# Own maxima for the last four pieces, a first load in halves, and a new step order in the prologue of an attention-plus-PReLU kernel

## The chip, the core and the metric

The kernel runs on one core of one Trainium2 chip. The metric is the device time of one execution in microseconds (us), the median of several runs. A core has five engines that work side by side, each through its own queue in program order: TensorE (PE: matrix products and transposes), VectorE (DVE), ScalarE (ACT), GpSimd (POOL), and SyncE (SP), which here only issues DMA transfers. 16 DMA engines move the data. Matrix products land in PSUM, from where DVE or ACT copy them to SBUF; POOL does not touch PSUM in this kernel.

## The reference

Two layers, one after the other. The first is attention through 32 learned rows I ("inducing"), for each of 4 batches of 12480 rows of 128 floats:

```python
def mab(q, kv):
    s = scale * (q @ kv.transpose(0, 2, 1))
    s = s - s.max(-1, keepdims=True)
    a = np.exp(s)
    a /= a.sum(-1, keepdims=True) + 1e-09
    return a @ kv
h = mab(I, x)       # 32 rows per batch, a softmax over all 12480 rows of x
y = mab(x, h)       # every row of x against these 32 rows
```

The second takes the 49920 rows of y through `h = y @ w_in` (128 to 2048 columns), `g = max(h, 0) + alpha * min(h, 0)`, and `g @ w_out` (2048 to 128). Inputs and output are float32; the kernel computes its products in bf16. The softmax of the first `mab` runs over a whole batch, so nothing of y can be computed for a batch before all of its 12480 rows have been read.

## The kernel before, in words

**Phase A and phase B.** Phase A of a batch is `h = mab(I, x)`. Phase B is everything after it for that batch: the second attention and the two products, in one main loop over blocks of 512 rows, four "visits" of 4 x 128 columns of w_in to each block (`visit`, `second`, `linear`, `finish`, L791 to L903). The main loop does phase B of batch b and, between its products, phase A of batch b + 1; a planner (`Plan`) settles before the build which of ACT and DVE does which evacuation. Only phase A of batch 0 has nothing to hide under. It is the **prologue**: an order of steps written out by hand (the string `order`, L1117 to L1125), which `begin` (L1045) carries out one by one. Every step puts its instructions at the end of the queue of the engine that it uses, so the string fixes the order on each engine.

**Pieces.** Batch 0 is read in eight pieces (`first_pieces`): piece 0 is 16 tiles of 128 rows, piece 1 the short rest of 192 rows, pieces 2 to 5 are 16 tiles each, and pieces 6 and 7 are the two halves (8 tiles each) of the last 16. A buffer holds 16 tiles (1 MB of float32) and there are four buffers (`xs`, bufs=4). The first five pieces are loaded at once; the load of piece 5 waits for the buffer of piece 0, those of pieces 6 and 7 for that of piece 2. The loads of `w_in` and `w_out` (1 MB each, `load_weights`, L1031) take the buffers of pieces 3 and 4. In `load_weights` a small POOL memset of two columns stands ahead of the load of `w_in` (L1033); the load waits for it, and it stands in POOL's queue behind the first POOL cast of piece 5.

**Steps of a piece p**, in the letters of the string, with a trailing a, v or p for ACT, DVE or POOL:

- `kp.i`: cast part i of the piece to bf16 (L347, L349; the short piece L335).
- `tp.i`, `cp.i`: transpose that part on PE (L364) and copy it from PSUM (L370, L372).
- `sp`: the scores of the piece against I (L379). `mp` (`a_least`, L388): one DVE scan negates and scales the scores and accumulates their minimum into column p of `mx` (L393), and a reduce over columns 0 to p gives the running minimum in column p of `rm` (L402).
- `ep` (`a_exp`, L413): ACT's exponential with `rm[p]` as bias, its sum in `da[p]`. `fp` (`a_fac`): the factor exp(rm[p] - rm[p-1]) on ACT (L436).
- `up`, `vp`: transpose the exponentials back (L456) and copy them (L462, L464).
- `hp`: PE's product with the piece (L473). `gp` (`a_add`, L483): DVE adds it to the running sum: hs = hs * fac[p] + product (L489).

After the last piece: `mg`, `rb`, `mm`, `mf` join the four groups of 32 partitions (L508, L517, L524/L525, L531); `ex` (`a_worth`, L544) gives each piece's weight exp(rm[last] - rm[p]), `dn` (`a_total`, L554/L555) the denominator, `pd`, `rec` its reciprocal (L568, L573/L574), `ph`, `hT` the result h transposed (L583, L588). From there the first block of phase B is made ready: `b`, `bm`, `bs`, `be`, `bt`, `ba` are scores, maximum, difference, exponential, transpose and copy of the first four tiles (L645, L676, L680, L774, L780, L788); `w`, `hw` are h times w_in (L599, L606); `b2`, `rx`, `rl`, `rk`, `re` do the scores of the other twelve tiles. Then visit 0 begins (L809, followed by `second`, L835).

**Weights.** `kwp` casts w_in on POOL (L1076). Right at that step SP's transpose of it, `winT` (L1135), is issued, and eight POOL products are queued: four make W1 from w_out (L974), which `second` needs, and four make AW (L983), which `linear_product` (L993) needs at visit 5. Batch 1's first loads follow `winT` in SP's queue.

**Zero products.** `Wn` and `warm(n)` (L956) put n products of a blank tile into PE's queue, 128x256 in bf16, each into a PSUM bank that nobody reads; 34 of them come before the first piece's transposes, 44 stand in the string.

**Banks.** `ring` gives the prologue's PSUM tiles out of six banks in turn.

## Time and profile before

| | |
|---|---|
| median of 3 runs | 592.18 us (592.09 to 592.28) |
| the profiled execution's own time | 592.11 us |
| span of its trace, first to last instruction | 590.3 us |
| granted TensorE clock over the span | 0.999 |
| PE's products over the whole span, `second` (L835) | 417.2 us |
| PE's products over the whole span, `visit` (L809) | 155.4 us |
| bytes moved over the span | 80.56 MB |

The trace is of one execution; all its times are counted from the first instruction. A row of the timeline gives the start, the duration, the engine, the line, the operation, the tiles written and read, their shapes and the number of merged instructions; a bracket at its end is the time that the engine sat idle before it and what ended that time. A merged row's duration runs from the first start to the last end. A row of the windows gives for each engine the busy time in a stretch, then the granted clock, the mean busy share of the 16 DMA engines, and the GB/s that they moved.

### The profile page before, as it was taken

To read this page: it belongs to the slowest core of one execution; us is meant where nothing else is said; L and a number is where in the kernel's file an instruction comes from. 1 tells how busy PE (TensorE), PEld (TensorE's weight loads), DVE (VectorE), ACT (ScalarE), POOL (GpSimd) and SP (SyncE) were. 2 spreads that over 40 slices of the span, in tenths; PEclk is the share of its full clock that TensorE was granted. 3 is DMA by queue.
4 is the path that set the end of the run, shared out by engine and by line. 5 is a ranking of instruction groups with operands and counts; after the bars stand their busy time and mean duration, and the time that the engine had idled before them with its cause. 6 is when DMAs were issued, how large, how long until landed. Compare 5 with 4: busy or idle time off the path is not lost.

```text
span 590.3 us, 23123 instructions
## 1 busy us (share of the span) xinstructions
PE 582.9 (99%) x9492; PEld 440.0 (75%) x9492; DVE 535.0 (91%) x979; ACT 537.6 (91%) x1087; POOL 217.1 (37%) x262
## 2 busy tenths in 40 slices
PE   9999999999999999999999999999999999999997
PEld 6577777777777777777777777777777777777776
DVE  5899999988998999999999899999999999999996
ACT  5799999999999999999999999999998998999986
POOL 3485552523325525413326256124034134144110
PEclk9999999999999999999999999999999999999999
DMA  8968699532188999332258899531331341433421
GB/s 336 276 181 176 158 250 197 132 98 73 39 240 159 209 216 222 94 95 58 78 152 181 194 255 204 136 100 38 92 77 50 92 81 49 118 85 57 92 69 47
DMA packets 122411, 80.56 MB, mean 136 GB/s; under 512 B 103824, under 2 KB 106176, under 8 KB 119232
## 3 DMA queue, kind: packets, MB, share of 16 engines
q1 hardware_dynamic: 122080, 78.99, 55.3%
q8 instruction: 74, 1.21, 0.8%
q14 instruction: 33, 0.27, 0.2%
q10 hardware_dynamic: 224, 0.09, 0.1%
HBM read 28.07 MB, written 25.56 MB: 91 GB/s over the span
## 4 chain that ended last, share of the span: by engine, by line
PE 95%; DMA 3%; DVE 1%; DVEq 0%; ACT 0%; issue 0%; POOL 0%; SPq 0%
PE bp L835 66%; PE hh L809 22%; DMA xs<-in_x_dram 3%; PE bp L862 2%; PE hh L645 2%; PE hh L473 1%; PE hh L379 1%; PE bp L960 0%; PE hh L364 0%; PE hh L599 0%; DVEq L1366 0%; PE hh L456 0%; DVE xn L349 0%; PE hh L583 0%; DVE hs L489 0%
## 5 line engine op out<-in xcount | busy, mean ns | idle before, releaser
L822 ACT ACTIVATE gt<-hh 128x512 bf16<-128x512 f32 x854 | 455.3, 606 | 34.4 <-PE hh L809 29.5
L824 DVE TENSOR_SCALAR gt<-hh 128x512 bf16<-128x512 f32 x706 | 453.7, 684 | 24.0 <-PE hh L809 13.6
L835 PE MATMUL bp<-W,gt 128*128 128x128 bf16 x6240 | 417.2, 220 | 0.7 <-DVE gt L824 0.7
L835 PEld LDWEIGHTS <-gt 128*128 128x128 bf16 x6240 | 349.4, 98 | 84.6 <-issue 76.0
L809 PE MATMUL hh<-a,HW 32*128 32x512 bf16 (+2 forms) x1664 | 155.4, 370 | 0.0
L759 POOL TENSOR_TENSOR rep<-e,rc 128x2048 bf16<-128x2048 f32 (+2 forms) x26 | 84.8, 3265 | 23.0 <-DVE rc L750 22.6
L727 POOL TENSOR_TENSOR e<-e,smx 128x512 f32<-128x512 f32 (+1 forms) x24 | 24.6, 1026 | 154.7 <-ACT gt L822 83.5
L809 PEld LDWEIGHTS <-HW 32*128 32x128 bf16 x1664 | 40.4, 91 | 41.6 <-issue 5.8
L713 POOL TENSOR_TENSOR t<-e 128x256 f32<-128x256 f32 (+1 forms) x24 | 17.2, 718 | 142.5 <-ACT e L689 142.5
L888 ACT COPY ob<-bp 128x512 f32<-128x512 f32 (+1 forms) x63 | 36.9, 586 | 4.5 <-PE bp L835 1.4
L713 POOL TENSOR_TENSOR t<-t 128x128 f32<-128x128 f32 (+3 forms) x100 | 30.5, 305 | 7.8
L330 POOL CAST xn<-xs 128x2048 bf16<-128x2048 f32 x17 | 32.1, 1890 | 0.8 <-DMA xs<-in_x_dram 0.3
L890 DVE COPY ob<-bp 128x512 f32<-128x512 f32 x31 | 21.3, 686 | 5.2 <-PE bp L835 5.2
L393 DVE TENSOR_SCALAR_CACHE_REDUCE s<-hh 128x512 f32<-128x512 f32 (+2 forms) x29 | 18.0, 619 | 1.6 <-PE hh L379 1.6
L862 PEld LDWEIGHTS <-a 32*128 32x128 bf16 x392 | 15.0, 93 | 5.7
L862 PE MATMUL bp<-HA,a 32*128 32x128 bf16 x392 | 19.1, 214 | 0.0
L418 ACT ACTIVATE e1T<-s,rm 128x512 bf16<-128x512 f32 (+1 forms) x25 | 18.0, 719 | 0.3
L722 DVE TENSOR_REDUCE smx<-e 128x16 f32<-128x512 f32 (+1 forms) x24 | 15.9, 662 | 0.0
L689 ACT ACTIVATE e<-e 128x512 f32<-128x512 f32 (+1 forms) x24 | 15.0, 624 | 0.0
L960 PE MATMUL bp<-blank 128*128 128x256 bf16 x78 | 13.6, 308 | 1.2 <-DVE blank L910 1.2
L489 DVE SCALAR_TENSOR_TENSOR hs<-hs,fac,hh 128x128 f32<-128x128 f32 (+1 forms) x25 | 8.6, 344 | 5.9 <-PE hh L473 5.2
L703 ACT COPY e<-hh 128x512 f32<-128x512 f32 (+1 forms) x22 | 13.4, 609 | 0.0
(107 smaller groups left out, 202.1 us busy)
## 6 DMA issues: line engine op xcount, KB each, us to landing
out_dram<-ob SPq DMA_DIRECT2D x97, 256.0 KB, 2.6
xs<-in_x_dram SPq DMA_DIRECT2D x23, 1024.0 KB, 6.1
xs<-in_x_dram SPq DMA_DIRECT2D x2, 512.0 KB, 9.2
w_in_f<-in_moe_w_in_dram SPq DMA_DIRECT2D x1, 1024.0 KB, 4.8
a<-rep SPq DMA_TRANSPOSE x27, 4.6
xT<-xn SPq DMA_TRANSPOSE x18, 5.7
e<-e1T SPq DMA_TRANSPOSE x18, 3.6
xs_left<-in_x_dram SPq DMA_DIRECT2D x4, 64.0 KB, 5.0
```

Source lines behind the costliest of these rows:

```text
L330: nc.gpsimd.tensor_copy(out=st.xn[s][:], in_=xs[:])
L393: nc.vector.tensor_scalar(out=s1[:parts, :cols], in0=ps[:parts, :cols], scalar1=-scale, scalar2=None, op0=MULT, op1=MIN, accum_out=st.mx[: ...
L713: nc.gpsimd.tensor_tensor(out=t[:, :n], in0=src[:, :n, :w], in1=src[:, :n, w : 2 * w], op=ADD)
L727: nc.gpsimd.tensor_tensor(out=st.e2[s][:, :n], in0=st.e2[s][:, :n], in1=st.m2[s][:, :n].unsqueeze(2).broadcast_to([P, n, M]), op=SUB,)
L759: nc.gpsimd.tensor_tensor(out=st.rep[s][:, ts], in0=st.e2[s][:, ts].unsqueeze(2).broadcast_to([P, n, R, M]), in1=rc[:, ts].unsqueeze(2).un ...
L809: nc.tensor.matmul(hh[:, q * cols + w.start : q * cols + w.stop], HWs[b][rows, v * P : (v + 1) * P], a2[rows, t0 : t0 + nt, :].rearrange(" ...
L822: nc.scalar.activation(out=gt[:, :cols], in_=hh[:, :cols], func=RELU)
L824: nc.vector.tensor_relu(gt[:, :cols], hh[:, :cols])
L835: nc.tensor.matmul(blk.acc[:, t * C : (t + 1) * C], gt[:, (q * nt + t) * P : (q * nt + t + 1) * P], W1[:, k, :], start=(not blk.begun), st ...
L862: nc.tensor.matmul(blk.acc[w, t * C : (t + 1) * C], blk.a2[rows, blk.t0 + t, w], HAs[b][rows, :], start=(not blk.begun and t == 0), stop=F ...
L888: nc.scalar.copy(out=ob[:, :nt], in_=acc)
L890: nc.vector.tensor_copy(out=ob[:, :nt], in_=acc)
```

## The change

- Pieces 4 to 7 of batch 0 (`own`) no longer take the running minimum: the scan's minimum goes straight into `rm[p]`, and the reduce over the columns is not issued for them. A new step `ml` (`a_lowest`) takes the minimum of `rm[3]` to `rm[7]` once, into `lo`. The factors `f4` to `f7` are gone; `g4` to `g7` use ex[p], the weight against `lo`, as factor of the new product instead of a factor of the sum, and a new step `gs` (`a_scale`) multiplies the sum of pieces 0 to 3 by ex[3] once, on POOL. `g4` to `g7` thus come after `ml` and `ex`. `dn` writes its products to a tile of its own (`dx`).
- Piece 0 is loaded in two halves, the second half first.
- The short piece is 2 x 96 rows in place of 128 + 64: one load and one cast in place of two of each, in every batch. Scores and exponentials of a piece take a view with a third dimension for it.
- The small memset ahead of the load of w_in is gone; the two loads of weights are issued at a new step `lw`.
- Zero products: a float32 blank of 512 columns. Ahead of the first piece's transposes stand two products of 512 columns and one of 384, each one instruction in the source; in the string stand one of 256, two of 128 and one of 256 columns (`W2`, `W1`, `W1`, `W2`).
- The eight POOL products of the weights are queued after the last step instead of at `kwp`; `winT` stays at `kwp`.
- The whole string is new.

```diff
@@ a_load
-            ts = slice(pc.t0, pc.t0 + pc.n)
-            nc.sync.dma_start(out=st.xs[s][:, ts], in_=rows[:, ts])
+            cut = pc.t0 + (H if not (st.b or pc.k) else 0)
+            for ts in (slice(cut, pc.t0 + pc.n), slice(pc.t0, cut)):
+                if ts.start < ts.stop:
+                    nc.sync.dma_start(out=st.xs[s][:, ts], in_=rows[:, ts])
...
+    def own(st, p):
+
+        return not st.b and p >= EARLY
+
+    def a_lowest(st):
+        nc.vector.tensor_reduce(
+            out=st.lo[:], in_=st.rm[:, EARLY - 1 : st.np], axis=AX, op=MIN
+        )
+
+    def a_scale(st):
+
+        nc.gpsimd.tensor_tensor(
+            out=st.hs[:],
+            in0=st.hs[:],
+            in1=st.ex[:, EARLY - 1 : EARLY].broadcast_to([P, C]),
+            op=MULT,
+        )
@@ a_least
-                accum_out=st.mx[:parts, p : p + 1],
+                accum_out=(st.rm if own(st, p) else st.mx)[:parts, p : p + 1],
             )
-            nc.vector.tensor_reduce(
-                out=st.rm[:, p : p + 1], in_=st.mx[:, : p + 1], axis=AX, op=MIN
-            )
+            if not own(st, p):
+                nc.vector.tensor_reduce(
+                    out=st.rm[:, p : p + 1], in_=st.mx[:, : p + 1], axis=AX, op=MIN
+                )
@@ a_add
+            elif own(st, p):
+                nc.vector.scalar_tensor_tensor(
+                    out=st.hs[:],
+                    in0=ps[:],
+                    scalar=st.ex[:, p : p + 1],
+                    in1=st.hs[:],
+                    op0=MULT,
+                    op1=ADD,
+                )
@@ blank and warm
-    blank = const.tile([P, 2 * P], bf16, name="blank")
-    for t in (xn_left, blank, e1T_left):
+    blank = const.tile([P, BT * P], f32, name="blank")
+    for t in (blank, xn_left, e1T_left):
...
-    def warm(n):
+    def warm(*widths):
 
         ps = ps_pool.tile([P, 512], f32, name="bp", tag=f"k{BANKS - 2}")
-        for _ in range(n):
-            nc.tensor.matmul(ps[:, : 2 * P], blank[:, :P], blank[:], start=True, stop=True)
-
-    warm(17)
+        for n in widths:
+            nc.tensor.matmul(
+                ps[:, : n * P], blank[:, :P], blank[:, : n * P], start=True, stop=True
+            )
+
+    warm(BT, BT)
     itp = ring([C, M], bf16)
...
-    warm(17)
+    warm(BT - 1)
@@ load_weights
-        nc.gpsimd.memset(kept["w_in"][:, :2], 0.0)
@@ order
-        k0.1v k0.2a t0.1 k0.0v t0.2 t0.0 c0.2a k1.0p c0.0v t1.0 c0.1a W5 s0 c1.0v s1
-        k2.2p m0 W5 t2.2 k2.0a m1 k2.1p W1 t2.0 c2.2v t2.1 al e0 c2.0v c2.1a u0 alc W3
-        s2 k3.0p e1 v0v k3.2p m2 k3.1p u1 v1a h0 f1 g0 e2 k4.0p W1 h1 k5.1p t3.0 t3.2
-        k5.2p u2 k4.2a k4.1a k6.1p g1 t3.1 W1 t4.2 v2a c3.0v c3.1v f2 t4.0 c3.2v c4.0a
-        t4.1 k5.0a s3 c4.2v c4.1v k6.0p m3 h2 W3 s4 t5.1 g2 W2 t5.2 k7.1p m4 e3 t5.0
-        c5.1a e4 k7.0p f4 om kwp t6.1 c5.2v c5.0v W2 t6.0 c6.1v s5 t7.1 u3 c6.0v t7.0 m5
-        c7.0v s6 u4 f3 c7.1a m6 v3a W1 h3 e5 v4v e6 s7 f5 m7 W2 u5 mg f6 h4 v5v g3 u6 e7
-        ex f7 g4 W1 h5 rb v6v u7 g5 v7a h6 mm mf dn g6 W2 h7 g7 pd rec W1 ph hT W4 b bm
-        b2 bs be w rx hw rl W5 re bt ba rk W5
+        k0.1a k0.2v k0.0v k1.0p t0.0 c0.0a t0.1 t0.2 t1.0 W2 c0.2v c1.0v k2.2p c0.1v k2.1v
+        k3.2p k3.1p s0 s1 k3.0p k2.0a m0 t2.1 t2.0 m1 e0 t2.2 u0 c2.0v c2.1a al c2.2v k4.2p
+        e1 s2 t3.2 u1 t3.1 alc m2 k5.1p f1 v0a h0 c3.2v v1a c3.1v e2 g0 f2 t3.0 k4.0v u2 h1
+        k4.1a v2a t4.0 c4.0a t4.1 k5.0a t4.2 g1 c3.0v s3 c4.1v lw c4.2v k5.2p s4 m3 m4 t5.1
+        k6.0p c5.1v t5.0 e3 t5.2 k6.1p f3 c5.2a k7.1p e4 u3 c5.0v h2 v3v t6.0 t6.1 s5 t7.1
+        c6.0a g2 c7.1a c6.1v k7.0p m5 t7.0 c7.0v e5 u4 s6 m6 s7 h3 m7 ml e6 u5 mg v4v ex g3
+        u6 v5v rb e7 h4 u7 gs mm om h5 kwp v6a h6 g4 dn g5 mf v7a g6 pd h7 W1 g7 ph W1 rec
+        hT b w bm bs b2 W2 be rx bt W2 rk ba rl hw re
@@ after a step
             nc.sync.dma_start_transpose(out=winT[:], in_=w_in_b[:])
-            for i in range(NV):
-                weights(i, nc.gpsimd)
-            for i in range(NV):
-                linear_weights(i)
+    for i in range(NV):
+        weights(i, nc.gpsimd)
+    for i in range(NV):
+        linear_weights(i)
```

More of the change, by code (lines that the diff above doesn't have):

```diff
@@ L58 @@
         nt = -(-left // P)
-        supers.append((len(supers) * ST * P, nt, left - (nt - 1) * P))
+        supers.append((len(supers) * ST * P, nt, left // nt))
     NS = len(supers)
@@ L77, in __init__ @@
             self.parts = P if self.full else M
-            self.cols = self.q * P if self.full else (n - 1) * P + supers[s][2]
+            self.last = supers[s][2]
+            self.cols = n * self.last if not self.full else self.q * P
             self.tile = tile0[s] + t0
@@ L91 @@
     NX = len(first_pieces)
+    EARLY = NX // 2
     const = ctx.enter_context(tc.tile_pool(name="const", bufs=1))
@@ L299, in new_state @@
         st.ex = sm_pool.tile([P, NX], f32, name="ex", tag="ex")
+        st.dx = sm_pool.tile([P, NX], f32, name="dx", tag="dx")
+        st.lo = sm_pool.tile([P, 1], f32, name="lo", tag="lo") if not b else st.rm[:, st.np - 1 : st.np]
         st.den = sm_pool.tile([P, 1], f32, name="den", tag="den")
@@ L313, in a_load @@
             rows = x[st.b, r0 : r0 + nt * P, :].rearrange("(p j) c -> p j c", p=P)
-            ts = slice(pc.t0, pc.t0 + pc.n)
-            nc.sync.dma_start(out=st.xs[s][:, ts], in_=rows[:, ts])
+            cut = pc.t0 + (H if not (st.b or pc.k) else 0)
+            for ts in (slice(cut, pc.t0 + pc.n), slice(pc.t0, cut)):
+                if ts.start < ts.stop:
+                    nc.sync.dma_start(out=st.xs[s][:, ts], in_=rows[:, ts])
         else:
             st.xs[s] = xs_left
-            for t in range(nt):
-                n = last if t == nt - 1 else P
-                nc.sync.dma_start(
-                    out=xs_left[:n, t, :], in_=x[st.b, r0 + t * P : r0 + t * P + n, :]
-                )
+            rows = x[st.b, r0 : r0 + nt * last, :].rearrange("(p j) c -> p j c", p=last)
+            nc.sync.dma_start(out=xs_left[:last], in_=rows)
     def a_cast(st, pc):
@@ L332, in a_cast @@
             st.xn[s] = xn_left
-            for t in range(nt):
-                n = last if t == nt - 1 else P
-                nc.gpsimd.tensor_copy(out=xn_left[:n, t, :], in_=xs[:n, t, :])
+            nc.gpsimd.tensor_copy(out=xn_left[:last], in_=xs[:last])
     def a_cast_part(st, pc, t0, n, eng):
@@ L418, in work @@
             nc.scalar.activation(
-                out=e1T[:parts, :cols],
-                in_=s1[:parts, :cols],
+                out=e1T[:parts, : pc.q * P].rearrange("m (j t) -> m j t", j=pc.q)[:, :, : pc.last],
+                in_=s1[:parts, :cols].rearrange("m (j t) -> m j t", j=pc.q),
                 func=EXP,
@@ L508, in work @@
             nc.scalar.activation(
-                out=st.mg[:], in_=group[:], func=COPY, scale=st.rm[:, st.np - 1 : st.np]
+                out=st.mg[:], in_=group[:], func=COPY, scale=st.lo[:]
             )
@@ L525, in a_factors_min @@
         nc.vector.tensor_tensor(
-            out=st.m2r[:], in0=st.m2r[:], in1=st.rm[:, st.np - 1 : st.np], op=SUB
+            out=st.m2r[:], in0=st.m2r[:], in1=st.lo[:], op=SUB
         )
@@ L1127 @@
     last_cast = {}
-    weights_after = next(step for step in order.split() if step[:2] == "k5" and step[-1] == "p")
     for step in order.split():
```

16 lines of the change are left out of this document (8 added, 8 removed).

## The prediction

> **What bounds the kernel now.** First two rows of the windows, one of the prologue and one of the main loop.
>
> ```profile
> 10.00:20.00 10.00, 8.70 (x136) 5.95 (x135) 7.77 (x28) 8.30 (x19) 5.56 (x10) 1.00 0.94 361
> ...
> 200.00:300.00 100.00, 100.00 (x1661) 75.65 (x1658) 92.37 (x170) 93.96 (x193) 39.10 (x43) 1.00 0.57 127
> ```
>
> The main loop keeps PE busy for 100.00 of 100 us. The diff leaves its visits and the planner's inputs alone; what changes there (one cast and one load less per batch for the short piece) is on POOL and SP, neither of which is near its limit. So nothing is to be won or lost after the prologue unless the prologue hands something over late, and the end moves by as much as visit 0 moves. Between 10 and 20 us, in contrast, the DMA engines are 94% busy and every other engine has gaps. POOL's timeline shows what the gaps wait for, PE's where the loop begins.
>
> ```profile
> 9.17 1.17 POOL L349 CAST xn<-xs 128x512 bf16<-128x512 f32 x2 [1.41 <-DMA xs<-in_x_dram]
> 11.66 2.16 POOL L349 CAST xn<-xs 128x1024 bf16<-128x1024 f32 x3 [1.32 <-DMA xs<-in_x_dram]
> 14.16 1.04 POOL L349 CAST xn<-xs 128x1024 bf16<-128x1024 f32 x1 [0.34 <-DMA xs<-in_x_dram]
> 17.92 0.62 POOL L349 CAST xn<-xs 128x512 bf16<-128x512 f32 x1 [2.72 <-DMA xs<-in_x_dram]
> ...
> 23.54 1.89 POOL L1076 CAST w_in_b<-w_in_f 128x2048 bf16<-128x2048 f32 x1 [1.74 <-DMA w_in_f<-in_moe_w_in_dram]
> 28.59 4.04 POOL L974 TENSOR_TENSOR W<-w_out_f,om_al 128x512 bf16<-128x512 f32 x4 [3.17 <-DMA w_out_f<-in_moe_w_out_dram]
> ```
> ```profile
> 30.08 0.40 PE L809 MATMUL hh<-a,HW 32*128 32x512 bf16 x4
> ```
>
> Pieces 2, 3 and 4 (1 MB each) arrive at 9.17, 11.66 and 14.16, 2.5 us apart. Piece 5 should follow at 16.7 and comes at 17.9; POOL had waited 2.72 us for it. Pieces 6 and 7 are cast without a real wait behind it. Visit 0 starts at 30.08. The prologue is thus two stretches: transfers until about 18 to 20 us, then a chain of computation. From 19.62 the engine of that chain is DVE:
>
> ```profile
> 19.62 1.80 DVE L372 COPY xT<-hh 128x512 bf16<-128x512 bf16 x4 [1.17 <-PE hh L364]
> 21.34 0.68 DVE L393 TENSOR_SCALAR_CACHE_REDUCE s<-hh 128x512 f32<-128x512 f32 x1
> ...
> 23.00 0.42 DVE L464 COPY e<-hh 128x512 bf16<-128x512 bf16 x1
> 23.36 0.42 DVE L393 TENSOR_SCALAR_CACHE_REDUCE s<-hh 128x256 f32<-128x256 f32 x1
> ...
> 24.95 0.28 DVE L464 COPY e<-hh 128x256 bf16<-128x256 bf16 x1
> ...
> 27.38 0.19 DVE L588 TENSOR_TENSOR hT<-hh,rec 128x32 bf16<-128x32 f32 x1
> ```
>
> It sat idle 1.17 us before 19.62, and from there to hT's end at 27.57 no row of it has a bracket. The marks that I use: the last landing (k7.1 on POOL), m7's scan at 23.36, hT's end at 27.57, visit 0 at 30.08.
>
> **Part 1: the landings, -1.2 us.** Why is piece 5 late? SP's timeline has the issue of piece 5 and, in a later stretch, those of pieces 6 and 7; the DMA view gives the time from issue to landing of pieces 5 and 6, and for 15 to 16 us the packets of the instruction queue; the windows give the products that PE had executed by then, and the DMA share just after the stream.
>
> ```profile
> 7.44 0.33 SPq L315 DMA_DIRECT2D xs<-in_x_dram  x1
> ```
> ```profile
> 10.37 0.80 SPq L315 DMA_DIRECT2D xs<-in_x_dram  x2
> 18.61 0.33 SPq L1034 DMA_DIRECT2D w_in_f<-in_moe_w_in_dram  x1
> ...
> 25.45 3.01 SPq L1135 DMA_TRANSPOSE winT<-w_in_b  x1
> 28.57 0.52 SPq L315 DMA_DIRECT2D xs<-in_x_dram  x1
> ```
> ```profile
> xs<-in_x_dram SPq DMA_DIRECT2D x1, 1024.0 KB, 10.4
> ```
> ```profile
> xs<-in_x_dram SPq DMA_DIRECT2D x1, 512.0 KB, 8.8
> ```
> ```profile
> q8 instruction: 1, 0.02, 6.9%
> ```
> ```profile
> 0.00:15.60 15.60, 14.16 (x149) 1.00 0.85 342
> ```
> ```profile
> 18.50:19.00 0.50, 0.41 (x6) 0.34 (x6) 0.00 (x0) 0.50 (x2) 0.50 (x3) 1.00 0.09 33
> ```
>
> Piece 5 lands at 7.44 + 10.4 = 17.8, piece 6 at 10.4 + 8.8 = 19.2, and piece 7, a half like it, some 1.25 us (half of 2.5) behind at about 20.4. But by 18.5 the DMA engines are 9% busy: one or two of 16 still work. So one lagging engine sets these three landings. In the slice from 15 to 16 a single packet of instructions took 6.9% of 16 engine-microseconds, that is 1.1 us of one engine, and about 1.1 is what piece 5 has lost (17.8 less 16.7). I read it as PE's next instructions being fetched on an engine that is also carrying x.
>
> PE had then executed 149 products. The new kernel reaches its 149th later: the 34 zero products ahead of the pieces become three, which I count as six (a float32 product leaves two rows, below), and the 16 of the string up to there become one, counted as two: 42 fewer. Counted along the new string, number 149 falls into h2, behind t5 and u3. These need piece 5, so h2 stands at about 18.7, when the stream of x is nearly over. Then pieces 5, 6, 7 land at about 16.6, 17.9 and 19.1: -1.2 us, my largest and least certain term. Bounds: 0 (the fetch is not the cause, or hits x again; nothing new stands ahead of x in SP's queue that could make it later) and -1.4 (with a little for the short piece, whose 192 packets of 512 bytes become 96).
>
> The Trainium skill ("Runtime: NRT & Kernel Launch", Instruction fetch mechanics) has an engine's instructions refilled in blocks of 256, 16 KiB, and calls the cost mostly hidden. The packet's 0.02 MB agrees with the block. By "mostly hidden" this term would be nothing and the time 591.8, the first rival below.
>
> The load in halves lets work on piece 0 start about 1.2 us earlier (half of 2.5); later landings cover it, but it pays for two casts that move onto DVE (k2.1v and k4.0v, one of each size that this row merges):
>
> ```profile
> 6.34 1.03 DVE L349 CAST xn<-xs 128x512 bf16<-128x512 f32 x2 [4.07 <-DMA xs<-in_x_dram]
> ```
>
> The dropped memset lets w_in go out some 5 us before 18.61, behind x in the same queue. Nothing waits for that: `kwp` now stands behind `gs` in POOL's queue.
>
> **Part 2: from the last landing to m7, -0.35 us.** Before: k7.1 can start at 20.4 and m7 starts at 23.36, 2.95 us. After, from 19.1: two casts of 0.62 (20.35), PE's transposes (four; about 0.4, as for visit 0's four products at 30.08), the copy (1.80 / 4 = 0.45, 21.2), scores and the hop to DVE (0.45): m7 at about 21.65, 2.6 us. What goes is the copy (v4) that stood between m6 and m7 (0.36 from 23.00 to 23.36). DVE must have caught up by then. Walking the new string by the rows' durations, it ends m4 at about 17.95 and c5.1 at 18.35, with some 0.3 us of gaps left since 8 us. That is tight, and a rival.
>
> **Part 3: from m7 to hT, 0.** Before: 27.57 - 23.36 = 4.21 us of DVE without a gap.
>
> ```profile
> L713 POOL TENSOR_TENSOR t<-t 128x128 f32<-128x128 f32 (+3 forms) x100 | 30.5, 305 | 7.8
> ```
>
> m7's reduce goes and `ml`, the same reduce, comes. The copy that no longer stands ahead of m7 (v4, 0.42) now stands behind it, and v6 (0.28 at 24.95) goes to ACT. Four `g` remain. Sum +0.1, against f5 to f7 gone from ACT: I take 0. The order has a new wait: g4 for `gs`, `gs` for `ex`, `ex` for `ml`; behind g4 on DVE stand dn, g5, g6, g7 and rec, so hT. `gs` is not in the trace; the nearest POOL row, also 128x128 float32, is L713's 305 ns, and I take that (ends: 0.2 by DVE's product of 128x32 at 27.38, and 1.0, a quarter of L974's 4.04, at four times the columns). It lies beside v5 (a copy of 128x512, 0.42) and mm (two small ones) and costs nothing; at 1.0 or without the cover it costs up to 0.7. `mg` and `ex` stand ahead of e7 on ACT where `mg` and a factor stood. `kwp` behind `gs` and the small `om`: 23.4 + 1.89 = 25.3, and `w` needs it after hT at 25.9: 0.6 us of cover; beyond it, `w` and b2 on PE would wait.
>
> **Part 4: from hT to visit 0, 0.** 30.08 - 27.57 = 2.51 us before. w now precedes b2 and rk stands ahead of ba (later), the zero products ahead of bt shrink (sooner); each shifts a queue by one small instruction.
>
> **What is late next?** Two rows, ACT's first cast for batch 1 and the landing of its load:
>
> ```profile
> 36.75 0.62 ACT L347 CAST xn<-xs 128x512 bf16<-128x512 f32 x1
> ```
> ```profile
> xs<-in_x_dram SPq DMA_DIRECT2D x1, 1024.0 KB, 5.6
> ```
>
> The load goes out 28.57 - 25.45 = 3.1 us behind `kwp`, whose end stays at 25.3 or 25.4, and lands at 28.5 + 5.6 = 34.1; the cast stands 36.75 - 30.08 = 6.7 us into the loop, then at 35.2. 1 us of cover is left. W1 follows w_out's landing, 28.59 before and by my estimate 26 when it goes out behind x without a pause: first quarter at 27.0 (4.04 / 4), needed about 1.5 us after visit 0, at 30; AW another 4.04 behind W1, at 34.1, needed after that cast.
>
> **The sum**: -1.2 - 0.35 = -1.55 on the profiled execution's 592.11 (a span of 590.3 and 1.8 around it), so 590.6. The median shown is 0.07 above that execution, well inside what I can resolve.
>
> **The rivals.**
>
> 1. *The landings stay* (the fetch is not what delays piece 5, or falls on x again). For it: the packet's engine can't be seen. Against: sizes and moment agree. Then only part 2 is left: 591.8.
>
> 2. *DVE takes the place of the transfers.* It gets 1.03 us of casts and has 0.3 us of gaps between 8 and 18 in my walk, where the old order left 1.17 in one piece. If the walk slips by 1 us, m7 starts at 22.65 and the time is 591.6.
>
> 3. *PE's clock, the slower side.* Two rows of PE's timeline, and one of its groups:
>
> ```profile
> 1.19 3.81 PE L960 MATMUL bp<-blank 128*128 128x256 bf16 x17 [1.19 <-DVE blank L910]
> ...
> 5.12 2.16 PE L960 MATMUL bp<-blank 128*128 128x256 bf16 x17
> ```
> ```profile
> L517 PE MATMUL hh<-mg,same 128*128 128x4 f32 x2 | 0.4, 262 | 0.0
> ```
>
> The first 17 zero products take 3.81 / 17 = 224 ns each, the next 17 127 ns: PE runs at about half speed until it has worked some 4 us. The new wide ones must do the same, and no row shows a float32 product of 512 columns. From below, at bf16's early rate, 448 ns each: 0.9 us, and the clock stays low. From above, at four times that: 3.6 us, as before. I take the upper end, as L517, one product in the source, leaves two records. If the clock is low until visit 0, seven PE steps on the chain (t7, s7, u7, h7, ph, b, bt) of about 0.4 us by visit 0's row grow by half, 1.4, and the first 3.9 us of visits run at half rate, 1.95: 590.6 + 3.35 = 594.0. It decides only if the real transposes and products between 8 and 24 us don't raise the clock by themselves.
>
> The Trainium skill ("TensorE: Matmul & The Clock Gate", Part 1) states a free-running window of 3.4 us, full clock after a busy one and half clock after an idle one. The 3.9 us from 1.19 to 5.12 agree. By that rule no gap of the new prologue is long enough to lose the clock, though an unaligned start could miss it at first.
>
> **How the numbers follow.** Forecast 0.50 (its own range 589.7 to 591.2), landings stay 0.22, DVE 0.13, clock 0.10, none of these 0.05. 0.2% is 1.2 us and about what a measurement of this kernel can tell from no change; faster by more means below 591.0. Faster: 0.47 of the forecast, 0.04 of DVE, 0.01: 0.52. Slower: the clock and 0.01: 0.11. Same: 0.37. The range, 589.7 to 592.4, leaves out the clock and the ends of the others, about 0.16.
>
> **What would show it.** Right: piece 5's first cast near 16.6 instead of 17.9; the instruction packet after 18; m7's scan near 21.65 with no copy ahead of it; hT's end near 25.85; visit 0 near 28.5, and the loop after it without new gaps. Wrong: PE's zero and real products after 8 us at the pace of the first 17 (clock); DVE without a gap from 8 to 18 and c5.1 far behind its transposes (DVE); `gs` waiting for `ex` while g4 waits; ACT waiting for batch 1's first load.

## The result, and the profile after

| | before | after |
|---|---|---|
| median, 6 runs each on one chip | 592.14 us (592.07 to 592.28) | 596.48 us (595.10 to 596.72) |
| the profiled execution's own time | 592.11 us | 595.10 us |
| span of its trace | 590.3 us | 593.1 us |
| mean granted TensorE clock, all runs | 0.999 in the profiled one | 0.993 to 0.996 |

After to before is 1.0068, with a 95% interval of 1.0055 to 1.0081. The change makes the kernel 4.3 us slower; the forecast was 1.5 us faster, and 596.48 lies outside its range.

The marks of the prediction, read from the profiled execution of the changed kernel (lines of the new file: casts L350, scan L412, `ml` L394, `gs` L400, own `g` L509, `dn` L583/L584, `pd` L597, `hT` L617, zero products L989, visits L838, `kwp` L1109):

| mark | before | forecast | after |
|---|---|---|---|
| piece 5's first POOL cast | 17.92 | 16.6 | 17.09 |
| start of the instruction packet | 15.4 to 15.6 | after 18 | 17.5 to 18.0 |
| m7's scan | 23.36 | 21.65 | 23.05 |
| end of hT | 27.57 | 25.85 | 28.98 |
| visit 0 | 30.08 | 28.5 | 32.54 |

POOL's timeline of the changed kernel, with the casts of pieces 5 to 7, `gs` and `kwp`:

```profile
17.09 2.46 POOL L350 CAST xn<-xs 128x512 bf16<-128x512 f32 x4 [1.34 <-DMA xs<-in_x_dram]
20.48 1.18 POOL L350 CAST xn<-xs 128x512 bf16<-128x512 f32 x2 [0.92 <-DMA xs<-in_x_dram]
24.42 0.40 POOL L400 TENSOR_TENSOR hs<-hs,ex 128x128 f32<-128x128 f32 x1 [2.76 <-DVE hs L518]
24.79 0.20 POOL L1110 TENSOR_SCALAR om_al<-alT 128x16 f32<-128x16 f32 x1
24.93 1.89 POOL L1109 CAST w_in_b<-w_in_f 128x2048 bf16<-128x2048 f32 x1
```

Piece 5 is 0.8 us earlier than before. Piece 7 is not: POOL now waits 0.92 us for it and casts at 20.48. Before, POOL cast pieces 5 to 7 back to back from 18.52 and never waited for piece 7. `kwp` runs from 24.93 to 26.82; before it ran from 23.54 to 25.43. SP's timeline has the issue of w_in's load (18.61 before), and the DMA view for 17 to 18 us has the packet that stood at 15.4 before:

```profile
14.31 0.33 SPq L1064 DMA_DIRECT2D w_in_f<-in_moe_w_in_dram  x1
```
```profile
q8 instruction: 1, 0.02, 6.9%
```

DVE's timeline over the time of `kwp`:

```profile
23.05 0.42 DVE L412 TENSOR_SCALAR_CACHE_REDUCE s<-hh 128x256 f32<-128x256 f32 x1
...
23.52 0.16 DVE L394 TENSOR_REDUCE lo<-rm 128x1 f32<-128x5 f32 x1
...
24.97 0.35 DVE L509 SCALAR_TENSOR_TENSOR hs<-hh,ex,hs 128x128 f32<-128x128 f32 x1
25.24 1.60 DVE L583 TENSOR_TENSOR dx<-ex,da 128x8 f32<-128x8 f32 x1
26.88 0.16 DVE L584 TENSOR_REDUCE den<-dx 128x1 f32<-128x8 f32 x1
...
28.79 0.19 DVE L617 TENSOR_TENSOR hT<-hh,rec 128x32 bf16<-128x32 f32 x1
```

The row to stop at is L583. An operation on 128x8 numbers takes 1.60 us, and no bracket stands behind it: nothing in the semaphores made it wait, so a list of waits doesn't show it. The source view of that line has the same product four times, once for each batch:

```profile
L583 DVE TENSOR_TENSOR dx<-ex,da x4: 167/168/1602, 25.2 to 398.5; 128x7 f32<-128x7 f32 x3, 128x8 f32<-128x8 f32 x1
```

Three take 167 or 168 ns; the one that began 0.31 us after POOL's cast ended at 26.84, with the cast (26.82). What hangs on it stands in PE's timeline and, microsecond by microsecond, in the windows (after the sum of each engine come the granted clock, the DMA share and the GB/s):

```profile
27.18 0.38 PE L597 MATMUL hh<-mf,den 128*128 128x32 f32 x2 [1.67 <-DVE den L584]
...
30.13 1.20 PE L989 MATMUL bp<-blank 128*128 128x256 f32 x2
...
32.54 0.40 PE L838 MATMUL hh<-a,HW 32*128 32x512 bf16 x4
```
```profile
25.00:26.00 1.00, 0.52 (x26) 0.34 (x24) 1.00 (x2) 0.53 (x2) 1.00 (x1) 1.00 0.13 35
26.00:27.00 1.00, 0.00 (x0) 0.00 (x0) 0.96 (x3) 0.00 (x0) 1.00 (x2) 1.00 0.00 0
...
28.00:29.00 1.00, 0.95 (x6) 0.67 (x6) 0.85 (x4) 0.00 (x0) 1.00 (x2) 0.81 0.90 172
29.00:30.00 1.00, 1.00 (x17) 0.48 (x16) 0.58 (x2) 0.00 (x0) 1.00 (x2) 0.50 1.17 216
...
31.00:32.00 1.00, 1.00 (x18) 0.54 (x18) 0.41 (x2) 0.00 (x0) 1.00 (x2) 0.50 0.84 254
32.00:33.00 1.00, 0.98 (x10) 0.36 (x14) 0.56 (x3) 0.35 (x2) 1.00 (x2) 0.98 0.98 393
```

PE stands still for 1.67 us (0.00 busy from 26 to 27), and some 1.4 us after it goes on, its clock falls to a half for 3.4 us (by the shares 0.81 and 0.98 of the first and last slice, from 28.6 to 32.0). That is the stretch in which block 0 is made ready and visit 0 begins.

By stages: up to m7 -0.31; m7 to hT 28.98 - 23.05 = 5.93 instead of 4.21, +1.72; hT to visit 0 32.54 - 28.98 = 3.56 instead of 2.51, +1.05. Together +2.46 at visit 0. The last output leaves at 589.73 instead of 586.94, +2.79, so 0.33 is lost inside the loop; 0.2 lies outside the span. That is the 2.99 us between the two profiled executions.

### The profile page after: what moved, and what is told of

Its sections match the earlier page's. It is cut to its first block, busy times and chain, and to the rows that moved or that the text cites. A ratio compares the mean times of both kernels' runs of the same rounds, so it can differ in the third digit from the quotient of the medians.

```text
span 593.1 us, 22984 instructions
## 1 busy us (share of the span) xinstructions
PE 581.0 (98%) x9430; PEld 436.2 (74%) x9430; DVE 537.0 (91%) x977; ACT 536.9 (91%) x1083; POOL 216.6 (37%) x257
## 4 chain that ended last, share of the span: by engine, by line
PE 94%; DMA 3%; DVE 1%; ACT 0%; issue 0%; SPq 0%; DVEq 0%; POOL 0%; ACTq 0%
PE bp L864 65%; PE hh L838 22%; DMA xs<-in_x_dram 3%; PE bp L891 2%; PE hh L674 2%; PE hh L493 1%; PE hh L380 1%; PE bp L989 0%; DVE dx L583 0%; PE hh L628 0%; ACT gt L851 0%; POOL xn L350 0%; SPq L321 0%; DVEq L1395 0%; ACT xn L348 0%
## 5 line engine op out<-in xcount | busy, mean ns | idle before, releaser
L851 ACT ACTIVATE gt<-hh 128x512 bf16<-128x512 f32 x854 | 455.3, 606 | 33.7 <-PE hh L838 28.6
L838 PE MATMUL hh<-a,HW 32*128 32x512 bf16 (+2 forms) x1664 | 155.7, 370 | 0.0
L838 PEld LDWEIGHTS <-HW 32*128 32x128 bf16 x1664 | 40.3, 91 | 41.7 <-issue 5.9
L412 DVE TENSOR_SCALAR_CACHE_REDUCE s<-hh 128x512 f32<-128x512 f32 (+2 forms) x29 | 17.9, 619 | 1.6 <-PE hh L380 1.3
L674 PE MATMUL hh<-hT,xT 128*128 128x32 bf16 x372 | 13.0, 177 | 0.0
L674 PEld LDWEIGHTS <-xT 128*128 128x128 bf16 x384 | 12.3, 96 | 0.7 <-issue 0.4
```

Of the source, the lines that this page charges most:

```text
L674: nc.tensor.matmul(ps[w, t, :], st.xT[:, tile0[s] + t, w], hTs[b][:], start=True, stop=True)
L838: nc.tensor.matmul(hh[:, q * cols + w.start : q * cols + w.stop], HWs[b][rows, v * P : (v + 1) * P], a2[rows, t0 : t0 + nt, :].rearrange(" ...
L851: nc.scalar.activation(out=gt[:, :cols], in_=hh[:, :cols], func=RELU)
```

## The experiments

**Theories.** *Collision*: DVE's product of two operands in SBUF (`dn`) stands still while POOL's cast of w_in runs; the change moved the cast onto it. *Clock*: few wide zero products leave PE gaps in which the granted clock falls, and this, not the held product, is what the time consists of. They exclude each other only as to size. A third question is why piece 7 did not land earlier: the *instruction packet*, or the *weights' load*, which the change sends out at 14.31 instead of 18.61.

Each run has the mean granted clock over its span beside its time. One stretch of 3.4 us at half clock takes 1.7 / 593 = 0.003 off that mean, so a mean of 0.997 or less, where 0.998 to 1.000 is normal, marks a run that lost the clock; it does not say where in the run. The kernel before, run beside the experiments, did so in 1 of 31, 2 of 31 and 2 of 29 runs (three chips; its medians there 592.16, 591.99 and 591.94 us). The ratios below are against these.

| kernel | median (lowest to highest), us | ratio, 95% interval | runs at 0.997 or less |
|---|---|---|---|
| the change as it is | 596.48 (595.10 to 596.72) | 1.0068, 1.0055 to 1.0081 | 6 of 6 |
| x1: no collision | 593.62 (592.27 to 596.56) | 1.0026, 1.0006 to 1.0046 | 5 of 10 |
| x2: PE's gap filled | 594.67 (594.07 to 595.29) | 1.0037, 1.0024 to 1.0050 | 0 of 10 |
| x3: both | 594.65 (594.02 to 597.78) | 1.0043, 1.0026 to 1.0060 | 1 of 10 |
| x4: before, cast later | 594.85 (591.84 to 596.06) | 1.0038, 1.0023 to 1.0054 | 7 of 10 |
| y4: before, cast held for mg | 592.73 (591.79 to 594.22) | 1.0014, 1.0003 to 1.0025 | 3 of 10 |
| y1: before, new loads | 592.69 (592.30 to 593.32) | 1.0008, 0.9998 to 1.0018 | 0 of 10 |
| y2: before, new zero products | 593.83 (591.72 to 596.99) | 1.0028, 1.0010 to 1.0046 | 6 of 10 |
| y3: before, own maxima | 591.99 (591.74 to 593.60) | 1.0000, 0.9991 to 1.0010 | 0 of 10 |
| z2: y3 with new zero products | 592.59 (592.19 to 594.51) | 1.0013, 1.0001 to 1.0025 | 6 of 10 |
| z3: x1, weights' load held | 593.10 (592.28 to 595.23) | 1.0021, 1.0011 to 1.0030 | 2 of 10 |
| z1: x1, old zero products | 593.26 (592.61 to 594.33) | 1.0018, 1.0007 to 1.0029 | 0 of 8 |
| z4: z1, weights' load held | 592.84 (592.70 to 594.60) | 1.0015, 1.0006 to 1.0025 | 0 of 10 |

### The held product

**x1** takes the product off DVE: POOL does it ahead of the cast, DVE keeps the sum.

```diff
-        nc.vector.tensor_tensor(out=st.dx[:, :n], in0=st.ex[:, :n], in1=st.da[:, :n], op=MULT)
+        nc.gpsimd.tensor_tensor(out=st.dx[:, :n], in0=st.ex[:, :n], in1=st.da[:, :n], op=MULT)
...
-        u6 v5v rb e7 h4 u7 gs mm om h5 kwp v6a h6 g4 dn g5 mf v7a g6 pd h7 W1 g7 ph W1 rec
+        u6 v5v rb e7 h4 u7 gs mm om dx h5 kwp v6a h6 g4 dn g5 mf v7a g6 pd h7 W1 g7 ph W1 rec
```

> The changed kernel, with dn's product of 128x8 moved from DVE to POOL, ahead of the cast of w_in. Theory: DVE's product with two SBUF operands was held by POOL's cast (1.60 us in place of 0.16), and the hole that this left on PE let its clock fall. Then no DVE row near 25 us lasts over 0.5 us, hT ends near 27.5 instead of 28.98, the granted clock stays 1.00 from 28 to 32 us, visit 0 starts near 30.0 instead of 32.54, and the time is about 592.2. Rival (the clock falls because too few zero products are left, stall or not): hT near 27.5, but the clock still falls, and the time is 593.5 to 595.

POOL's and DVE's timelines of x1:

```profile
25.04 0.20 POOL L583 TENSOR_TENSOR dx<-ex,da 128x8 f32<-128x8 f32 x1
25.18 1.89 POOL L1115 CAST w_in_b<-w_in_f 128x2048 bf16<-128x2048 f32 x1
```
```profile
25.33 0.15 DVE L589 TENSOR_REDUCE den<-dx 128x1 f32<-128x8 f32 x1
```

The sum of one operand (L589) runs beside the cast in 0.15 us. hT ends at 27.59, visit 0 stands at 30.06 (before: 30.08), and the median is 2.9 us below the change's. But the runs scatter by 4.3 us, with the clock: the five at 0.999 or 1.000 take 592.27 to 593.68, the five at 0.996 or less 593.57 to 596.56. So the theory was right on the held product, and the rival on the clock, in half of the runs.

**x4 and y4** go the other way. In the kernel before, the cast ends at 25.43 and mm's subtraction, the next product of two SBUF operands on DVE, starts at 25.62: 0.19 us apart. Both hold the cast back with a POOL copy of 128x1, x4 until e7's sum is there, y4 until `mg`:

```diff
+            "kg": lambda: nc.gpsimd.tensor_copy(out=st.gate[:], in_=st.mg[:, 0:1]),
...
-        c5.1a e4 k7.0p f4 om kwp t6.1
+        c5.1a e4 k7.0p f4 om t6.1
-        ... u5 mg f6 h4 v5v g3 u6 e7
+        ... u5 mg kg kwp f6 h4 v5v g3 u6 e7
```

(In x4 the copy reads `st.da[:, 7:8]`, and `kg kwp` stand behind `e7`.)

> The kernel before, with POOL's cast of w_in held back until e7's sum is there, so that it covers dn's product. Theory: dn or the product ahead of it lasts until the cast ends, over 1 us in place of 0.16, and the time grows by 1 to 3 us (stall, and the clock if PE's hole is long enough): 593.2 to 595. Rival (own maxima or the new order are the cause): the rows of dn stay at 0.16 and the time at 592.1 to 592.4.

> The kernel before, with the weights' cast on POOL held back by a copy of 128x1 that waits for mg, so that the cast begins between 24.4 and 25.2 us and covers DVE's dn near 25.7 us, which in the kernel before it misses by 0.27 us. Nothing else is changed. Theory (the cast holds DVE's product of two operands in SBUF until it ends): dn takes 0.8 to 1.7 us instead of 0.16 us in the trace, hT's end is later by as much, PE is idle over 1 us, and the time is 593.5 to 595.5 us. Rival (dn's 1.60 us in the changed kernel came of its waits or its order): dn takes 0.16 us beside the cast and the time stays at 592.0 to 592.3 us.

x4's profiled execution, at 591.84 its fastest, is one that missed: POOL waited another 0.66 us for w_in, and the cast began 0.05 us after the product had ended.

```profile
25.61 1.89 POOL L1078 CAST w_in_b<-w_in_f 128x2048 bf16<-128x2048 f32 x1 [0.66 <-DMA w_in_f<-in_moe_w_in_dram]
```
```profile
25.40 0.16 DVE L555 TENSOR_TENSOR ex<-ex,da 128x8 f32<-128x8 f32 x1
```

The other nine runs take 593.41 to 596.06, but have no trace. Two of them, at 0.998 and 0.999, take 593.58 and 593.41, 1.4 and 1.25 us over the kernel before and about what a held product alone would add (1.60 us instead of 0.17); the seven at 0.997 or less take 594.47 to 596.06. y4's trace has the collision, with mm's subtraction of a single column in place of `dn`:

```profile
24.09 1.90 POOL L1078 CAST w_in_b<-w_in_f 128x2048 bf16<-128x2048 f32 x1
```
```profile
25.19 0.80 DVE L526 TENSOR_TENSOR m<-m,rm 128x1 f32<-128x1 f32 x1
25.92 0.15 DVE L555 TENSOR_TENSOR ex<-ex,da 128x8 f32<-128x8 f32 x1
```
```profile
27.00:28.00 1.00, 0.94 (x13) 0.80 (x14) 0.65 (x4) 0.00 (x0) 0.00 (x0) 1.00 0.75 145
28.00:29.00 1.00, 1.00 (x21) 0.53 (x18) 0.84 (x3) 0.22 (x1) 0.89 (x1) 0.52 1.16 215
29.00:30.00 1.00, 1.00 (x5) 0.47 (x4) 0.50 (x2) 0.87 (x3) 1.00 (x2) 0.50 1.48 227
```

One number per partition takes 0.80 instead of 0.16 us and ends at 25.99, where the cast ends. hT comes only 0.21 us later than before (27.78), yet visit 0 comes 1.58 later (31.66): the clock falls here too, with all the old zero products in place, after `pd` had waited 0.70 us. The median, 592.73, is below what I expected; three of ten runs lost the clock, at 593.74 to 594.22. So *collision* holds as to mechanism, and in y4's trace the half clock behind it is the dearer part: 1.37 of the 1.58 us.

The Trainium skill ("SBUF — State Buffer", Who interferes with whom) gives DVE and GpSimd one pair of ports in common, locked for a whole instruction, and says that a DVE instruction with two SBUF inputs contends with a GpSimd instruction that reads SBUF. The rows agree: L583 and L526 wait, while g4 (L509, one operand in PSUM) at 24.97 and the sums of one operand run beside the cast in their usual time.

### The clock

**x2** leaves the collision and puts two zero products of 512 columns into PE's gap, **x3** does the same to x1.

```diff
-        ... v6a h6 g4 dn g5 mf v7a g6 pd h7 W1 g7 ph W1 rec
+        ... v6a h6 g4 dn g5 mf v7a g6 W4 W4 pd h7 W1 g7 ph W1 rec
```

> The changed kernel, with two zero products of 512 columns in PE's queue ahead of pd, where PE sat idle for 1.67 us. Theory: the stall of dn stays at 1.6 us and hT ends near 29.0, but the clock holds 1.00; visit 0 near 31.5 instead of 32.54, the time about 593.8. Rival (the clock falls for another reason): visit 0 near 32.5, time 595 to 596.5 as the changed kernel.

> Both edits. Theory: as with POOL's product alone, about 592.2, since without the stall the zero products have no hole to fill; they may delay pd by up to 1 us. Rival (too few zero products): clearly faster than with POOL's product alone, since only here the clock holds.

DVE's and PE's timelines of x2:

```profile
25.43 1.60 DVE L583 TENSOR_TENSOR dx<-ex,da 128x8 f32<-128x8 f32 x1
...
28.37 0.35 DVE L509 SCALAR_TENSOR_TENSOR hs<-hh,ex,hs 128x128 f32<-128x128 f32 x1 [0.43 <-PE hh L493]
```
```profile
25.64 2.31 PE L989 MATMUL bp<-blank 128*128 128x512 f32 x4
...
31.96 0.40 PE L838 MATMUL hh<-a,HW 32*128 32x512 bf16 x4
```

The product is still held for 1.60 us, but no run lost the clock: from hT's end (29.49) to visit 0 it is 2.47 us again, as before the change (2.51). The median falls by 1.8 us although the zero products, 2.31 us where some 1.7 would have done, hold g7 for 0.43; hT and visit 0 come some 0.5 later than I expected. x3, without a collision, pays for them in full and ends where x2 does, which neither the theory nor the rival had. Filling a gap is free only as long as the filling is no longer than the gap.

**y2** and **z2** give only the change's zero products to the kernel before and to y3 (below); **z1** gives x1 the old ones.

```diff
-    blank = const.tile([P, 2 * P], bf16, name="blank")
+    blank = const.tile([P, BT * P], f32, name="blank")
...
-    warm(17)
+    warm(BT, BT)
...
-    warm(17)
+    warm(BT - 1)
```

(The string keeps `W2` behind t1.0, b2 and bt, and `W1` behind h7 and ph; these five are what the changed kernel has, one `W2` more than the list of the change names. z1 is the reverse, with `W1` to `W5` at 17 places.)

> The kernel before with the change's zero products alone: two of 512 float32 columns and one of 384 at the start, and later only one or two of 256 columns in five places (behind t1.0, h7, ph, b2 and bt) in place of the many small ones. Theory (the many small products are what holds the granted clock between 8 us and the visits): a trace with a clock under 0.97 in some stretch of 10 to 36 us, or runs spread over 2 us, and a median of 593 to 596 us. Rival (the clock is not at stake so long as no wait of PE is longer than before's longest): clock 1.00 throughout, 592.0 to 592.3 us with a spread under 0.5 us.

> The kernel before with the own maxima (the weights' cast behind dx on POOL, so that no cast lies over DVE's joins), which took 592.0 us with its old zero products, and now with the change's zero products alone added to it: three wide float32 ones at the start, W2 or W1 in five places. Theory (the zero products are the part that loses the clock): several runs with a mean clock of 0.997 or less and 593.5 to 596 us, a median of 592.8 to 594.5 us. Rival (the clock fell only where DVE was held by the cast): mean clock 0.998 or more in every run, a median of 591.8 to 592.2 us.

> The changed kernel with dn's product on POOL ahead of the weights' cast (no collision), and with the zero products of the kernel before in place of the change's: 17 and 17 of 256 bf16 columns at the start and one to five of them at 15 places, behind the like steps. Theory (what spreads the runs of the changed kernel from 592.3 to 596.6 us, once the collision is gone, is the granted clock, and many small zero products hold it): mean clock 0.998 or more in every run, times within 1 us of each other, a median of 592.2 to 592.8 us. Rival (the spread comes of something else in the new order or the loads): runs up to 595 us remain.

In y2 and z2 6 of 10 runs each lost the clock; in y3, which is z2 with the old products, none. z1 and z4, which are x1 and z3 with the old products, lost it in none of 18 runs, x1 and z3 in 7 of 20. That is the *clock* theory, at a smaller price in z2 (592.59; I had put it at 592.8 or more): four of z2's six take 592.19 to 592.67, no more than those that kept the clock (592.20 to 593.00). Where it fell in them no trace shows. The wide start and the few later products always come together here, so which of the two loses the clock is not separated. In y2's profiled execution w_in landed at 24.22 (before: 23.54), so its cast met mm too, and its median mixes the two:

```profile
24.22 1.89 POOL L1078 CAST w_in_b<-w_in_f 128x2048 bf16<-128x2048 f32 x1 [2.62 <-DMA w_in_f<-in_moe_w_in_dram]
```
```profile
25.39 0.73 DVE L525 TENSOR_TENSOR m<-m,rm 128x1 f32<-128x1 f32 x1
```

PE's timeline and the windows of the same trace show what the clock fell behind:

```profile
26.54 0.40 PE L568 MATMUL hh<-mf,den 128*128 128x32 f32 x2 [0.25 <-ACT mf L531]
```
```profile
27.00:28.00 1.00, 0.81 (x6) 0.64 (x7) 0.78 (x4) 0.00 (x0) 0.34 (x1) 0.80 0.57 112
```

It fell at 27.6 and stayed at half until 31.0, and from 22 us on PE had not stopped for longer than the 0.25 us ahead of pd. So a long stop is not what it takes.

z1 held the clock but took 593.26, not 592.2 to 592.8. Its landings (below) are part of that: z4, with the weights' load held back, takes 0.42 less, but the rest stays.

### The landings

**y1** is the kernel before with the new loads (halves, 2 x 96 rows, no memset); **z3** and **z4** put the memset ahead of the weights' load back into x1 and z1.

```diff
         kept["w_in"] = xs_pool.tile([C, DFF], f32, name="w_in_f", tag="xs")
+        nc.gpsimd.memset(kept["w_in"][:, :2], 0.0)
         nc.sync.dma_start(out=kept["w_in"][:], in_=moe_w_in)
```

> The kernel before with the change's loads alone: the first piece in two halves, the short piece as two tiles of 96 rows with one load and one cast, the memset ahead of the weights' load gone; the zero products, the maxima and the order of the steps stay. Theory (what is loaded earlier waits for the instruction fetch, so the last landing does not move): the cast of piece 7 still waits until about 20.4 us, m7's scan stays at 23.2 to 23.4 us, the time is 592.0 to 592.3 us. Rival (the forecast's first part: the landings come 0.8 to 1.2 us earlier once the first loads are re-cut): piece 7's cast near 19.5 us and the time 591.0 to 591.4 us.

> The changed kernel with dn's product on POOL, and with the small memset ahead of the weights' load put back, so that w_in goes out when POOL has cast piece 5's first part (about 17.5 us) and not at 13.7 to 14.3 us. Theory A (w_in's packets share the DMA engines with pieces 6 and 7 and make them late): piece 7's cast starts at 19.7 us or earlier instead of 20.5, m7's scan at 22.3 us or earlier, and the fastest runs 0.5 us or more below the 592.3 us of the same kernel without the memset. Theory B (the instruction packet at 17.7 us alone makes them late): piece 7's cast stays at 20.4 to 20.6 us, m7 at 23.0 us, and the fastest runs stay at 592.3 us.

> Both of the edits above: the changed kernel with dn's product on POOL, the zero products of the kernel before, and the weights' load held back by the memset. If theory A on the landings and the theory on the clock both hold: a median of 591.2 to 591.8 us, below the kernel before. If theory B on the landings holds: 592.2 to 592.6 us. If the clock theory fails: a spread over 2 us as before.

The half microsecond in which the 16 KB instruction packet started (it took 1.1 us of one engine: 13.8% of 16 x 0.5), against the POOL casts of pieces 5 to 7 (each row from the timeline of the kernel named above it). y1, packet 14.5 to 15.0:

```profile
18.15 3.70 POOL L347 CAST xn<-xs 128x512 bf16<-128x512 f32 x6 [3.01 <-DMA xs<-in_x_dram]
```

y2, packet 16.5 to 17.0:

```profile
16.51 0.62 POOL L349 CAST xn<-xs 128x512 bf16<-128x512 f32 x1 [1.47 <-DMA xs<-in_x_dram]
...
18.96 2.46 POOL L349 CAST xn<-xs 128x512 bf16<-128x512 f32 x4 [1.24 <-DMA xs<-in_x_dram]
```

z3, packet 17.5 to 18.0, w_in sent out at 17.45:

```profile
16.77 0.61 POOL L350 CAST xn<-xs 128x512 bf16<-128x512 f32 x1 [1.37 <-DMA xs<-in_x_dram]
...
20.70 1.17 POOL L350 CAST xn<-xs 128x512 bf16<-128x512 f32 x2 [1.48 <-DMA xs<-in_x_dram]
```

Read down: a packet at 15 makes piece 5 late, at 16.5 piece 6, at 17.5 piece 7. All fourteen traces follow it: with the packet ahead of 16 (seven) piece 5's first cast stands at 17.45 to 18.15, with it at 16.5 to 17 (y2, z2) at 16.33 and 16.51 and piece 6 waits, with it behind 17 (the change, x1, x2, x3, z3) at 16.49 to 17.09 and piece 7 waits. That the packet is the cause is read from this order; no run moved it by itself. In each case the pieces ahead of it arrive at the old 2.5 us pace (16.3 to 17.1 for piece 5), the piece that it falls on is about 1.1 us or more late, and none of the three brings m7 more than 0.3 us forward (y1 23.57, y2 23.14, z3 23.27, before 23.36). z3 speaks against the weights' load as the cause: w_in went out at 17.45 instead of 13.67 in x1, and piece 7 was cast at 20.70 and 20.57. It isn't innocent everywhere: z1 (packet at 15.5, w_in out at 15.16) and z4 (the same packet, w_in out at 18.70) differ in that load alone:

```profile
21.70 1.17 POOL L350 CAST xn<-xs 128x512 bf16<-128x512 f32 x2 [1.13 <-DMA xs<-in_x_dram]
```
```profile
18.62 3.10 POOL L350 CAST xn<-xs 128x512 bf16<-128x512 f32 x5
```

In z1 POOL waits 1.13 us for piece 7, in z4 not at all, and z4's hT ends 1.03 earlier. What decides when the two loads disturb each other is open. z4 still took 592.84, above the 592.6 that I had set as the end of theory B, and not below the kernel before. y1 by itself can't be told from the kernel before; its visit 0 stands 0.20 later, at 30.28, and its median, 592.69, lies above the 592.0 to 592.3 that I expected.

### The own maxima alone

**y3** is the kernel before with `own`, `ml`, `gs` and dx on POOL, `f4` to `f7` gone, and `kwp` behind dx.

```diff
-        ... e6 s7 f5 m7 W2 u5 mg f6 h4 v5v g3 u6 e7
-        ex f7 g4 W1 h5 rb v6v u7 g5 v7a h6 mm mf dn g6 W2 h7 g7 pd rec W1 ph hT W4 b bm
+        ... e6 s7 m7 ml W2 u5 mg ex h4 v5v g3 u6 e7
+        W1 rb v6v u7 gs dx kwp h5 mm g4 g5 v7a h6 mf dn g6 W2 h7 g7 pd rec W1 ph hT W4 b bm
```

> The kernel before with the own maxima of pieces 4 to 7 alone: f4 to f7 are gone, ml, gs and own g4 to g7 are in, dn's product is a step of its own on POOL (dx), and the weights' cast on POOL stands behind it, so that nothing on DVE with two operands in SBUF stands beside the cast but mm's subtraction of one column. Loads, zero products and the order of the other steps stay. Theory (the own maxima are worth what part 2 said, about 0.3 us, and cost nothing else when the cast does not meet dn): m7's scan at 23.0 to 23.1 us, visit 0 at 29.6 to 30.1 us, 591.6 to 592.2 us. Rival (the joined factors are themselves a loss: gs ahead of g4 holds DVE): hT over 4.5 us behind m7, 592.8 us or more.

DVE's timeline of y3, then PE's:

```profile
23.08 0.42 DVE L414 TENSOR_SCALAR_CACHE_REDUCE s<-hh 128x256 f32<-128x256 f32 x1
...
27.30 0.19 DVE L624 TENSOR_TENSOR hT<-hh,rec 128x32 bf16<-128x32 f32 x1
```
```profile
29.99 0.40 PE L845 MATMUL hh<-a,HW 32*128 32x512 bf16 x4
```

m7 is 0.28 us earlier, hT 0.08, visit 0 0.09, and the time is the same (1.0000, 0.9991 to 1.0010). These are the marks that I expected, but not for my reason. Piece 7's first cast began at 20.18 instead of 20.44, and x4, with the running minima and the cast at 20.18 too, has m7 at 23.07: the 0.28 is the landing's. In y3 the copy v4 still stands between m6 and m7, so the own maxima gain nothing there, and from m7 to hT they cost 0.2 (4.41 us, against 4.21 before and 4.20 in x4's trace). y3 is the best version found; none is faster than the kernel before.

## Why the prediction was wrong

**Part 3 was wrong, and it turned the sign.** The step that failed is the sentence "`kwp` behind `gs` and the small `om`: 23.4 + 1.89 = 25.3, and `w` needs it after hT at 25.9: 0.6 us of cover". It asked who waits for the cast, never what the cast does to DVE beside it. The cast ran from 24.93 to 26.82 and not from 23.4 to 25.3, but nearly all of that is m7, which came 1.40 later than forecast (part 1): counted from m7, the cast began 1.88 us behind it, forecast 1.75, and `dn` stood 2.19 behind. So `dn` would have lain under the cast by the forecast's own times too. Worth: `dn` 1.60 instead of 0.16, +1.44, of the +1.72 in this stage. The other 0.28 has no stall: x1 and y3, without it, need 4.45 and 4.41 us from m7 to hT against 4.21. In y3 only the own maxima and the moves that go with them are new, so about 0.2 is the price of joining four pieces late, which I took as 0. The wait priced most carefully, g4 for `gs`, cost nothing: `gs` took 0.40 (estimate 0.305) and g4 started at 24.97.

**Part 4 and rival 3: the clock.** I had priced the low clock as one that never rises after the start, and by 5 us it had risen: from 5.11 on, a record of 384 columns takes 0.46 us, where 512 columns take 0.58 at full clock (x2). It was lost at 28.6 instead, behind a stop of PE that the rival didn't contain: +1.05 from hT to visit 0, where part 4 had 0. With the clock held, part 4 was right (2.47 us in x2, 2.51 before). The bound of the start was right at its upper end:

```profile
1.45 3.60 PE L989 MATMUL bp<-blank 128*128 128x512 f32 x4 [1.45 <-DVE blank L939]
```

The Trainium skill ("TensorE: Matmul & The Clock Gate", Part 1) has half clock after an idle window of about 3.4 us, a window that runs free of the kernel. Its length is what the traces show for the half clock (28.6 to 32.0 here, 28.0 to 31.5 in y4), and a free phase would fit runs of one kernel that fall or don't. But no PE gap here was that long: the clock fell behind 1.67 us in the change, 0.70 in y4 and 0.25 in y2. So the prediction's "no gap of the new prologue is long enough to lose the clock", drawn from that rule, fell.

**Part 1: piece 5 moved, the last landing did not.** -0.8 of the -1.2 came for piece 5, none of it for piece 7. The reading that the packet sits on one DMA engine fits every trace; whose instructions it carries, none shows. The count did not fit: product 149 fell into h2 as counted (at 19.2 to 19.5), but the packet started between 17.5 and 18.0, when PE had executed 125. And the reasoning had a gap of its own. In these traces a packet anywhere ahead of the last landing makes the last landing late; moving it from 15.5 to 17.5 changed only which piece pays. This is rival 1 ("or falls on x again", 591.8), as far as m7 goes: 23.05, about before's 23.36 less **part 2**'s 0.35. Part 2 was right: from piece 7's first cast to m7 it is 2.57 us (20.48 to 23.05, and as much in x1 and z3) instead of 2.92 (20.44 to 23.36), forecast 2.6. Rival 2, DVE's backlog, was not seen: DVE had waited 0.87 us ahead of piece 7's copy.

**What I said was untouched, the loop, lost 0.4.** DVE's reciprocals give two points in the loop that can be compared, in the kernel before, in x1 and in y3:

```profile
63.33 0.24 DVE L750 RECIPROCAL rc<-den 128x16 f32<-128x16 f32 x1
...
85.18 0.24 DVE L750 RECIPROCAL rc<-den 128x16 f32<-128x16 f32 x1
```
```profile
63.45 0.24 DVE L784 RECIPROCAL rc<-den 128x16 f32<-128x16 f32 x1
...
85.70 0.24 DVE L784 RECIPROCAL rc<-den 128x16 f32<-128x16 f32 x1
```
```profile
63.24 0.24 DVE L786 RECIPROCAL rc<-den 128x16 f32<-128x16 f32 x1
...
85.15 0.24 DVE L786 RECIPROCAL rc<-den 128x16 f32<-128x16 f32 x1
```

x1 goes from +0.12 to +0.52 between them, y3 stays (-0.09, -0.03). The change, x2, x3, z1, z3 and z4 show the same 0.4, the kernels with the old string do not, so it belongs to the new string or to the place where the weights' products are queued. In x1 DVE waits 0.56 us for a copy on ACT at 73.20; why, no run tells. With it x1's undisturbed runs add up: visit 0 as before and 0.4 in the loop make 592.16 + 0.4 = 592.6, against 592.3 to 592.5 in its three fastest.

**The size.** From the medians: the collision goes with 2.9 of 4.3 us (x1), part of it as clock; the clock alone with 1.8 (x2, which pays 0.43 for its filling). The two overlap, and the shares can't be split further, since the collision makes the gap in which the clock falls.

## What to carry to other kernels

When an instruction is moved on one engine, look at what then stands beside it on the others, not only at who waits for its result: here a POOL cast of 1.9 us that had missed DVE's small products by 0.19 us was moved onto one of them. A tiny operation that ends only when its neighbour on another engine ends, with no wait shown, is the sign. When filling products are thinned out, price PE's clock as well: in y4 the half clock cost 1.37 us and the held product ahead of it 0.21, and in y2 it fell with no stop of PE over 0.25 us. And compare a stage from its own start: y3's earlier m7 was an earlier landing.

## What the runs showed of the hardware

- A stop of PE of 0.70 us in a chain of small products was followed by 3.4 us at half clock (y4), at 0.997 or less in 3 of 10 runs. In y2's trace it fell with no stop over 0.25 us in the 5 us ahead. x1's profiled execution stood idle from 19.90 to 21.24 us and kept its clock. Nor is it PE's busy share: 2.68 of the 3.40 us ahead of the fall in y2, and 1.89 of 3.40 (19.0 to 22.4) without a fall in x1. What counts as idle isn't settled.
- In four of x1's ten runs 2.6 to 3.0 us, not 1.8 to 2.1, lie outside the span; 2.5 to 2.9 also in some runs of the change, x3, y2, z2 and z3, all with the wide float32 zero products at the start, and in none of the kernel before (1.7 to 1.9 in 91 runs). The trace doesn't reach there, and the cause is open.
- Two float32 products of 128x512 leave four records and took 3.60 us at the start of the program and 2.31 us at full clock (x2): 1.8 and 1.15 us each. The windows give the granted clock as 1.00 over the first 6 us in all fourteen traces, also where these products, and the first 17 of the kernel before (224 ns instead of 127), run slowly: that column does not record the slow start.
